# Ordering GpSimd behind VectorE on the shared SBUF port in an attention and MoE kernel

## The chip, the cores and the metric

The kernel runs on one core of a Trainium2 chip. Its time is device time in microseconds (us). Five engines work side by side, each through its own row of instructions: TensorE (PE) for matrix products, VectorE (DVE), ScalarE (ACT), GpSimd (POOL), and SyncE (SP), which here issues DMAs. They wait for each other by semaphores.

## What is computed

Three layers follow each other. The functions of the reference are cut to their cores:

```
# attention with random features, 4 x 8 heads, 576 tokens, 64 wide, 128 features
phi(x) = exp(h - max(h)) / sqrt(m),  h = x @ omega.T - sum(x * x) / 2
kv = phi(k).T @ v;  z = sum(phi(k));  attn = (phi(q) @ kv) / (phi(q) @ z + 1e-6)
# gated layer, 2304 tokens, 512 -> 1536 -> 512
x = (sigmoid(attn @ w_gate) * (attn @ w_val)) @ w_out
# soft mixture: 8 experts with 4 slots each, 512 -> 1024 -> 512
d = softmax(x @ phi, over tokens);  slots = d.T @ x
y = relu(slots[e] @ w1[e]) @ w2[e];  out = softmax(x @ phi, over slots) @ y
```

## The kernel before

The tokens are cut into five blocks of 512 (the last of 256), the gated layer's 1536 columns into twelve chunks. Attention works on 16 units of two heads each (tags `g...`, written to `XT`). For the gated layer each block runs over the chunks: twelve products of 512 columns for the gate (`ga`), twelve for the value (`va`), twelve for the product with w_out (`o`). The mixture's sums are built while later blocks run; its experts come last, from about 635 us.

Products of the gated layer are made of three passes. Each operand is split in a high part (`hi_of`: a copy in a shorter format, on ACT or DVE) and a low part (`lo_of`: a subtraction, mostly on POOL). So before PE can use a weight tile `w`, ACT copies its high part and POOL subtracts the low one. The same is done for `XT`, the attention's output, and for `gt`, the gated values.

During the first 225 us the weights also arrive as 64-bit floats and are converted once (`convert`): two instructions on ACT, then on DVE two TENSOR_SCALAR, one SCALAR_TENSOR_TENSOR (all on `x2T`) and an integer add (`x<-x2T`) that DVE or POOL may make. 36 tiles pass through this, while attention runs too. For the first units POOL also squares the tokens (`g<-g`), which are then summed by DVE.

All of it is recorded first and ordered afterwards. `Plan.schedule` is a planner that runs a list of times: each instruction has a due time, a cost from `Plan.cost`, and the engines on which it may run. `cost` returns a second value, whether the instruction holds the SBUF port that DVE and POOL share: true for every POOL instruction, and for DVE's copies, casts, TENSOR_SCALAR, TENSOR_TENSOR and SCALAR_TENSOR_TENSOR that have no operand in PSUM. While one such instruction is planned to run, `pick` offers the other engine only work that doesn't use the port. `Plan.issue` (line 402) then emits the instructions in the planned order. Each engine keeps that order, but the engines are tied together by data alone: semaphores are set where one reads or overwrites what another wrote. If DVE is behind the plan, POOL goes ahead of it. Nearly all instructions are emitted in line 405, so this line says nothing and the tiles tell the rows apart.

Of the kernel before, what the change touches and what calls it, by code (L numbers as in the profile page):

```python
# [103 lines left out]
class Plan:  # L104
# [294 lines left out]
        assert len(order) == n, (len(order), n)  # L399
        return order  # L400

    def issue(self):
        for _, _, (e, method, a, k) in self.schedule():
            for e, method, a, k in [p[0] for p in k["parts"]] if method == "together" else [(e, method, a, k)]:
                getattr(self.eng[e], method)(*a, **k)  # L405


def body(ctx, tc, nc, qkT, tok, von, omT, wall, phi, w1, w2, ident_d, srep_d, rrep_d, mask_d, out):
    plan = Plan(nc)
    PE, ACT, DVE, POOL, SP = (Eng(plan, e) for e in ("PE", "ACT", "DVE", "POOL", "SP"))  # L410
# [849 lines left out]
    i = 0  # L1260
# [50 lines left out]
        plan.t += 2.0  # L1311
        combine(half, po)
    with tc.manual_schedule():
        plan.issue()


def layout(q, k, v, omega, moe_w_gate, moe_w_val, moe_w_out, moe2_phi, moe2_w1, moe2_w2):
# [42 lines left out]
def build(nc, arrays):  # L1360
    args = [nc.dram_tensor(n, a.shape, mybir.dt.from_np(a.dtype), kind="ExternalInput").ap()
            for n, a in arrays.items()]
    args.append(nc.dram_tensor("out_0", (NTOK, DM), F32, kind="ExternalOutput").ap())
    with tile.TileContext(nc, schedule_with_timeline_sim=True) as tc:
        with ExitStack() as ctx:
            body(ctx, tc, nc, *args)
# [8 lines left out]
```

## Time and profile before

| | us |
|---|---|
| median of 3 runs | 690.68 (690.0 to 691.18) |
| profiled execution, its own time | 688.92 |
| its span in the trace | 687.1 |
| PE busy | 663.6 (97%) |
| DVE busy | 457.7 (67%) |
| ACT busy | 429.0 (62%) |
| POOL busy | 288.7 (42%) |

The span is what the trace covers; the time of the same execution is 1.8 us longer. Busy shares are averages over stages with different limits, and a PE that is busy may still be waiting between two matmuls for less than the trace counts as idle. A row of the timeline has the start in us from the span's start, the duration, the engine, the operation and its tiles (out<-in), shapes and count, and in brackets the idle time of the engine before it and what ended it. Rows of equal instructions that follow each other are put together with one count. [...]

### The profile page before, as it was taken

The page shows a single profiled execution, that of the slowest core. Times are in us where ns is not written, and L with a number is a line of the kernel's source. Part 1 is how long each engine was busy: PE and PEld are TensorE (multiplying, and loading weights), DVE is VectorE, ACT ScalarE, POOL GpSimd, SP SyncE. Part 2 cuts the span into 40 slices and gives each one's busy share as a digit, 9 for nine tenths or more (in the row PEclk, how much of TensorE's full clock was granted, in tenths as well). Part 3 has the DMA queues.
Part 4 walks back from the last instruction along what each step waited for, and adds up shares of the span by engine and source line. Part 5 has one row for each costly group of instructions (what it writes and reads, how often), then busy time and mean ns, then how long its engine had stood idle before and what let it go on. Part 6 is the DMA issues. An engine that isn't in the chain of part 4 may idle for free.

```text
span 687.1 us, 12505 instructions
## 1 busy us (share of the span) xinstructions
PE 663.6 (97%) x4366; PEld 533.8 (78%) x4366; DVE 457.7 (67%) x1299; ACT 429.0 (62%) x962; POOL 288.7 (42%) x245
## 2 busy tenths in 40 slices
PE   7999899999999999999999999999999999999994
PEld 5676577778787888788788888788888789999672
DVE  3899999899997575666666555567444335666413
ACT  5899788888787574766566675554344445675002
POOL 0566445565334343434444543434444444553100
PEclk9999999999999999999999999999999999999997
DMA  8889766777965336443444222589622328666978
GB/s 288 314 271 326 264 208 225 264 251 245 325 239 164 114 125 217 137 133 111 136 155 152 78 62 78 159 299 321 217 93 91 101 71 292 211 203 213 404 287 275
DMA packets 50158, 139.50 MB, mean 203 GB/s; under 512 B 5552, under 2 KB 11184, under 8 KB 50096
## 3 DMA queue, kind: packets, MB, share of 16 engines
q1 hardware_dynamic: 45488, 121.94, 52.2%
q10 hardware_dynamic: 4608, 16.78, 7.2%
q8 instruction: 34, 0.56, 0.3%
q14 instruction: 28, 0.23, 0.1%
HBM read 124.54 MB, written 14.16 MB: 202 GB/s over the span
## 4 chain that ended last, share of the span: by engine, by line
PE 77%; DVE 12%; DMA 4%; ACT 2%; issue 2%; SPq 1%; POOL 0%; DVEq 0%; ACTq 0%
PE o L405 24%; PE ga L405 19%; PE va L405 19%; PE fl L405 15%; DVE x2T L405 4%; DVE g L405 3%; DVE x L405 2%; DMA wscr<-x 1%; DMA g<-in_von 1%; DVE g1b L405 1%; DMA g<-in_tok 1%; ACT ga_a L405 1%; DMA ws<-wscr 1%; DVE ga_a L405 1%; ACT g L405 1%
## 5 line engine op out<-in xcount | busy, mean ns | idle before, releaser
L405 POOL TENSOR_TENSOR w<-ws,w 128x512 fp32r<-128x512 f32 x138 | 181.4, 1315 | 253.2 <-ACT w L405 157.1
L405 PE MATMUL ga<-XT,w 128*128 128x512 f32 (+1 forms) x720 | 168.2, 376 | 1.0 <-DVE ga_a L405 0.9
L405 PE MATMUL va<-XT,w 128*128 128x512 f32 (+1 forms) x720 | 167.3, 375 | 0.4 <-DVE ga_a L405 0.4
L405 PE MATMUL o<-gt,w 128*128 128x512 f32 (+1 forms) x720 | 167.2, 376 | 0.0
L405 PEld LDWEIGHTS va<-XT,w 128*128 128x128 f32 x720 | 123.8, 189 | 26.1 <-issue 3.2
L405 PEld LDWEIGHTS ga<-XT,w 128*128 128x128 f32 x720 | 123.6, 189 | 25.9 <-DVE ga_a L405 1.8
L405 PEld LDWEIGHTS o<-gt,w 128*128 128x128 f32 x720 | 123.5, 189 | 25.3 <-issue 3.9
L405 ACT ACTIVATE w<-ws 128x512 fp32r<-128x512 f32 x107 | 67.2, 628 | 59.4 <-PE o L405 18.9
L405 PE MATMUL fl<-g,g 64*128 64x128 f32 (+4 forms) x686 | 83.8, 313 | 4.9 <-DVE g L405 2.8
L405 ACT ACTIVATE g<-g 128x128 f32<-128x128 f32 (+3 forms) x204 | 73.3, 411 | 14.1 <-DVE g L405 9.1
L405 PEld LDWEIGHTS fl<-g,g 64*128 64x128 f32 (+2 forms) x686 | 60.8, 182 | 26.6 <-DVE g L405 9.1
L405 ACT ACTIVATE ga_a<-ga_a 128x512 f32<-128x512 f32 (+1 forms) x120 | 70.0, 583 | 18.0 <-DVE ga_a L405 17.0
L405 ACT ACTIVATE ga_a<-ga 128x512 f32<-128x512 f32 (+1 forms) x60 | 33.2, 553 | 67.9 <-PE ga L405 67.8
L405 DVE SCALAR_TENSOR_TENSOR ga_a<-ga,ga_a 128x512 f32<-128x512 f32 (+1 forms) x60 | 38.0, 634 | 39.1 <-ACT ga_a L405 39.0
L405 DVE CAST w<-ws 128x512 fp32r<-128x512 f32 x55 | 23.5, 428 | 59.7 <-PE ga L405 41.1
L405 DVE TENSOR_TENSOR ga_a<-va,ga_a 128x512 f32<-128x512 f32 (+1 forms) x60 | 38.1, 634 | 18.7 <-ACT ga_a L405 13.2
L405 ACT ACTIVATE x2T<-g 128x512 f32<-128x512 f32 x72 | 45.5, 665 | 7.8 <-DVE x L405 7.8
L405 ACT ACTIVATE g1b<-g1b,g 128x128 f32<-128x128 f32 x128 | 40.4, 389 | 8.6 <-DVE g L405 8.6
L405 DVE TENSOR_SCALAR x2T<-x2T 128x512 f32<-128x512 f32 (+1 forms) x72 | 44.9, 640 | 0.7 <-ACT x2T L405 0.6
L405 DVE TENSOR_TENSOR gt<-ga_a,gt 128x512 fp32r<-128x512 f32 (+1 forms) x52 | 41.9, 805 | 2.3 <-ACT gt L405 1.3
L405 ACT ACTIVATE ga_a<-ga_a,one_b 128x512 f32<-128x512 f32 (+1 forms) x60 | 40.7, 679 | 2.7 <-issue 1.4
L405 DVE TENSOR_TENSOR g<-fl,g 64x288 f32<-64x288 f32 (+3 forms) x61 | 29.4, 483 | 17.1 <-ACT g L405 16.2
(196 smaller groups left out, 808.0 us busy)
## 6 DMA issues: line engine op xcount, KB each, us to landing
ws<-wscr SPq DMA_DIRECT2D x42, 512.0 KB, 3.6
ws<-wscr SPq DMA_DIRECT2D x78, 256.0 KB, 2.8
g<-in_wall SPq DMA_DIRECT2D x36, 512.0 KB, 4.4
g<-in_von SPq DMA_DIRECT2D x16, 640.0 KB, 6.0
wscr<-x SPq DMA_DIRECT2D x36, 256.0 KB, 3.9
g<-in_qkT SPq DMA_DIRECT2D x15, 576.0 KB, 4.9
g<-in_tok SPq DMA_DIRECT2D x15, 576.0 KB, 4.7
g<-in_w ACTq DMA_DIRECT2D x16, 512.0 KB, 6.0
```

The costliest lines, as they stand in the source:

```text
L405: getattr(self.eng[e], method)(*a, **k)
```

## The change

`issue` now keeps, for each of the two engines, the last emitted instruction that holds the port. When it emits a POOL instruction on the port, and a DVE instruction on the port has been emitted since the last POOL instruction that took one, it adds a dependency: POOL waits for this DVE instruction. Nothing is added in the other direction; DVE never waits for POOL because of the port.

```
--- before.py
+++ after.py
@@ -399,10 +399,18 @@
         assert len(order) == n, (len(order), n)
         return order
 
-    def issue(self):
-        for _, _, (e, method, a, k) in self.schedule():
+    def issue(self, tc):
+
+
+        held = {}
+        sync = mybir.DependencyInfo(mybir.DependencyClass.Sync, mybir.DependencyReason.SCHED_ONLY)
+        for _, i, (e, method, a, k) in self.schedule():
             for e, method, a, k in [p[0] for p in k["parts"]] if method == "together" else [(e, method, a, k)]:
-                getattr(self.eng[e], method)(*a, **k)
+                ins = getattr(self.eng[e], method)(*a, **k)
+            if self.cost(e, method, k, self.ops[i][4], self.ops[i][5])[1]:
+                if e == "POOL" and "DVE" in held:
+                    tc.add_manual_dep(ins.ins, held.pop("DVE").ins.name, sync, reason="port")
+                held[e] = ins
 
 
 def body(ctx, tc, nc, qkT, tok, von, omT, wall, phi, w1, w2, ident_d, srep_d, rrep_d, mask_d, out):
@@ -1311,7 +1319,7 @@
         plan.t += 2.0
         combine(half, po)
     with tc.manual_schedule():
-        plan.issue()
+        plan.issue(tc)
 
 
 def layout(q, k, v, omega, moe_w_gate, moe_w_val, moe_w_out, moe2_phi, moe2_w1, moe2_w2):
```

No engine's row of instructions changes; what changes are the semaphores that stand before POOL's. Here are the rows of POOL at 172 to 216 us, with the semaphores that each waits for, before (`w` is the low part of a weight tile, `ws` its source, `g_78` squares of tokens, `XT` the attention's output; the names in brackets are the engines' semaphores, DMAHW a DMA's):

```order
L405 TENSOR_TENSOR w_269<-ws,w_269 128x512 [waits DMAHW3_49,Activation_49]
L405 TENSOR_TENSOR w_272<-ws,w_272 128x512 [waits DMAHW6_49,PE_49,Activation_49]
L405 TENSOR_TENSOR w_275<-ws,w_275 128x512 [waits Activation_49]
L405 TENSOR_TENSOR w_277<-ws,w_277 128x512 [waits DMAHW1_49,Activation_49]
L405 TENSOR_TENSOR w_282<-ws,w_282 128x512 [waits DMAHW4_49,PE_49,Activation_49]
L405 TENSOR_TENSOR w_285<-ws,w_285 128x512 [waits Activation_49]
L405 TENSOR_TENSOR w_287<-ws,w_287 128x512 [waits DMAHW7_49,Activation_49]
L405 TENSOR_TENSOR w_295<-ws,w_295 128x512 [waits DMAHW3_49,Activation_49]
L405 TENSOR_TENSOR g_78<-g_78 128x512 [waits DVE_49]
L405 TENSOR_TENSOR w_297<-ws,w_297 128x512 [waits DMAHW6_49,Activation_49]
L405 TENSOR_TENSOR w_303<-ws,w_303 128x512 [waits DMAHW3_49,PE_49,Activation_49]
L405 TENSOR_TENSOR XT<-g_80,XT 128x288 [waits Activation_49]
```

and the same rows of POOL after the change:

```order
L409 TENSOR_TENSOR w_269<-ws,w_269 128x512 [waits DMAHW3_49,DVE_49,Activation_49]
L409 TENSOR_TENSOR w_272<-ws,w_272 128x512 [waits DVE_49,DMAHW6_49,PE_49,Activation_49]
L409 TENSOR_TENSOR w_275<-ws,w_275 128x512 [waits DVE_49,Activation_49]
L409 TENSOR_TENSOR w_277<-ws,w_277 128x512 [waits DMAHW1_49,DVE_49,Activation_49]
L409 TENSOR_TENSOR w_282<-ws,w_282 128x512 [waits DVE_49,DMAHW4_49,PE_49,Activation_49]
L409 TENSOR_TENSOR w_285<-ws,w_285 128x512 [waits DVE_49,Activation_49]
L409 TENSOR_TENSOR w_287<-ws,w_287 128x512 [waits DMAHW7_49,DVE_49,Activation_49]
L409 TENSOR_TENSOR w_295<-ws,w_295 128x512 [waits DMAHW3_49,DVE_49,Activation_49]
L409 TENSOR_TENSOR g_78<-g_78 128x512 [waits DVE_49]
L409 TENSOR_TENSOR w_297<-ws,w_297 128x512 [waits DMAHW6_49,DVE_49,Activation_49]
L409 TENSOR_TENSOR w_303<-ws,w_303 128x512 [waits DVE_49,DMAHW3_49,PE_49,Activation_49]
L409 TENSOR_TENSOR XT<-g_80,XT 128x288 [waits DVE_49,Activation_49]
```

The order is the same, and eleven of the twelve now wait for DVE as well.

## Rows read from the trace of the kernel before

**Rows 1.** The page's first part: busy us (share of span) and instructions.
```profile
PE 663.6 (97%) x4366; PEld 533.8 (78%) x4366; DVE 457.7 (67%) x1299; ACT 429.0 (62%) x962; POOL 288.7 (42%) x245
```

**Rows 2.** Stretches of 25 us: their length, busy us (instructions) by engine, PEclk, DMA.
```profile
175.00:200.00 25.00, 23.83 (x125) 19.18 (x124) 24.93 (x51) 19.95 (x41) 8.67 (x7) 1.00 0.80 281
...
475.00:500.00 25.00, 25.00 (x140) 20.38 (x139) 13.12 (x27) 11.43 (x20) 11.61 (x9) 1.00 0.67 238
```

**Rows 3.** PE's waits, 25 to 225 us: total us, times, longest.
```profile
PE fl L405 <- DVE g L405: 5.7, 7, 1.7
PE ga L405 <- DVE ga_a L405: 0.7, 1, 0.7
PE o L405 <- DVE g L405: 0.5, 1, 0.5
```

**Rows 4.** PE's timeline at six of these waits.
```profile
79.98 0.37 PE L405 MATMUL fl<-g,g 64*128 64x128 f32 x1 [0.24 <-DVE g L405]
...
85.02 0.38 PE L405 MATMUL fl<-g,g1b 128*128 128x128 f32 x1 [1.70 <-DVE g L405]
...
104.44 0.38 PE L405 MATMUL fl<-g,g 128*128 128x128 f32 x1 [0.32 <-DVE g L405]
...
185.41 0.33 PE L405 MATMUL fl<-ident,g 128*128 128x128 f32 x1 [0.53 <-DVE g L405]
...
189.25 0.33 PE L405 MATMUL fl<-ident,g 128*128 128x128 f32 x1 [0.64 <-DVE g L405]
...
209.44 0.51 PE L405 MATMUL fl<-g,g 128*128 128x288 f32 x1 [1.65 <-DVE g L405]
```

**Rows 5.** DVE's groups by shape, 50 to 225 us: count, busy us, mean ns, idle before.
```profile
L405 DVE CUSTOM_DVE_ANT_0 x<-x2T 128x1024 uint16<-128x1024 uint16 x24 | 23.4, 975 | 0.1
L405 DVE TENSOR_SCALAR x2T<-x2T 128x512 f32<-128x512 f32 x32 | 20.8, 661 | 0.0
...
L405 DVE CUSTOM_DVE_ANT_0 g1b<-fl,g 128x128 f32<-128x128 f32 x48 | 10.6, 281 | 0.5 <-PE fl L405 0.5
```

**Rows 6.** DVE's and POOL's timeline, 174 to 189 us.
```profile
174.01 0.68 DVE L405 CUSTOM_DVE_ANT_0 x<-x2T 128x1024 uint16<-128x1024 uint16 x1
...
182.40 1.78 DVE L405 CUSTOM_DVE_ANT_0 x<-x2T 128x1024 uint16<-128x1024 uint16 x1
184.10 0.41 DVE L405 TENSOR_SCALAR x2T<-x2T 128x512 int32<-128x512 int32 x1
184.44 0.28 DVE L405 CUSTOM_DVE_ANT_0 g1b<-fl,g 128x128 f32<-128x128 f32 x1
...
186.85 1.79 DVE L405 CUSTOM_DVE_ANT_0 x<-x2T 128x1024 uint16<-128x1024 uint16 x1
...
182.07 1.55 POOL L405 TENSOR_TENSOR w<-ws,w 128x512 fp32r<-128x512 f32 x1 [2.94 <-ACT w L405]
186.80 1.30 POOL L405 TENSOR_TENSOR w<-ws,w 128x512 fp32r<-128x512 f32 x1 [3.18 <-ACT w L405]
```

**Rows 7.** DVE's timeline before the two longest waits.
```profile
80.94 3.19 DVE L405 TENSOR_SCALAR x2T<-x2T 128x512 f32<-128x512 f32 x3
...
206.64 1.78 DVE L405 CUSTOM_DVE_ANT_0 x<-x2T 128x1024 uint16<-128x1024 uint16 x1
```

**Rows 8.** POOL, DVE and PE around 164 us.
```profile
164.22 1.74 POOL L405 TENSOR_TENSOR w<-ws,w 128x512 fp32r<-128x512 f32 x1
...
167.03 1.52 DVE L405 TENSOR_SCALAR x2T<-x2T 128x512 f32<-128x512 f32 x1
...
168.22 2.88 PE L405 MATMUL o<-gt,w 128*128 128x512 f32 x12
```

**Rows 9.** POOL, DVE and PE around 58 us.
```profile
57.78 1.07 POOL L405 TENSOR_TENSOR XT<-g,XT 128x224 fp32r<-128x224 f32 x1
...
59.09 0.81 DVE L405 CUSTOM_DVE_ANT_0 x<-x2T 128x1024 uint16<-128x1024 uint16 x1
...
60.01 0.63 PE L405 MATMUL ga<-XT,w 128*128 128x512 f32 x2
```

## The prediction

> **What bounds the kernel now.** I read four views in this order: the page's busy times, the stretches of 25 us, the waits of TensorE, and the rows of VectorE and GpSimd around the places where TensorE stands still. TensorE (PE) is busy 97% of the span [rows 1], so only what it loses can be won. The stretches show where it loses. From 475 to 500 us, as in nearly every stretch from 225 to 575, PE is busy 25.00 of 25.00 us and VectorE (DVE) only 13.12: there PE sets the pace, and a later GpSimd (POOL) instruction costs nothing as long as PE's next input is ready. From 50 to 225 us it is the other way round: in the stretch from 175 DVE is busy 24.93 us and PE 23.83 [rows 2]. This is where weights are converted and two things share VectorE: conversion and attention.
>
> The waits say the same. Between 25 and 225 us PE waits 5.7 + 0.7 + 0.5 = 6.9 us for DVE, in nine places [rows 3]; six of them, from 80 to 210 us, sum to 0.24 + 1.70 + 0.32 + 0.53 + 0.64 + 1.65 = 5.08 us [rows 4]. So the question is why DVE is late in these six places.
>
> It is late because some of its instructions take over a microsecond longer than they need. The correction step (x<-x2T, the custom add) takes 0.68 us where nothing else touches the port [rows 6], but 975 ns on average over its 24 instances between 50 and 225 us; TENSOR_SCALAR on x2T, 0.41 us alone [rows 6], takes 661 [rows 5]. The long instances are all of one kind: POOL has begun a TENSOR_TENSOR a moment before. POOL starts at 186.80 and takes 1.30 us; DVE's add starts at 186.85 and takes 1.79 instead of 0.68, that is, it ends 0.54 us after POOL does [rows 6]. So DVE stands for the whole of POOL's instruction. If DVE is first, POOL pays, and far less: POOL's instruction that began at 182.07, during a DVE instruction, took 1.55 us against 1.30 [rows 6].
>
> **What the change does, and its price.** No instruction is added, removed or moved to another place in its engine's row; POOL gets waits. Of its 245 instructions 97 wait for DVE before and 183 after. The wait is for the DVE instruction on the port that stands just ahead in the plan. I set beside each POOL start in the trace the end of the DVE instruction it will wait for, plus 0.08 us, which is what passes in this trace between the end of a DVE instruction and the start of a POOL instruction that waited for it: 68 POOL instructions would start at least 0.1 us later, 38 of them between 50 and 225 us, by up to 6.3 us. The other new waits are over when POOL comes to them and cost nothing.
>
> *Gain on DVE.* Take the two collisions shown. POOL's instruction of 182.07 (its next DVE instruction, 182.40, took 1.78 us) and that of 186.80 will wait for the DVE instruction behind the blocked one. So both adds take 0.68 us, and DVE is 2 x 1.10 = 2.20 us ahead. Then POOL runs. Whether DVE now stands for it, one instruction later, depends on what DVE has next. At 184.44 come seven custom instructions of 0.28 us that read PSUM (g1b<-fl) [rows 6]; instructions that read PSUM are not lengthened in this trace (the average of the 48 such instances between 50 and 225 us is 281 ns [rows 5]). They cover POOL's 1.3 us. At 80.94 it is the same, and larger: three TENSOR_SCALARs take 3.19 us instead of 3 x 0.41 while POOL runs four instructions [rows 7]; POOL's first will come after all three, under eight custom instructions. At 206.64 the add takes 1.78 us behind POOL [rows 7]; that POOL instruction will wait for a later add, at 209.91. Each of the six waits of PE has 1.0 us or more of such loss in the ten or so DVE instructions before it, the longest (1.70 us) has the 3.19 us of these rows. I count 71 DVE instructions that lose over 0.2 us at the port, 50 us together; 25 of them, 22 us, are blocked by a POOL instruction that will now wait for them or for a later one. That is four times PE's six waits.
>
> *Gain on PE.* I take the six waits as gone: 5.08 us. Each costs a little more than its idle time: 12 matmuls of 512 columns in a row take 2.88 us and a single one 0.38, so they start (2.88 - 0.38) / 11 = 0.23 us apart [rows 8], and 0.15 us of overlap is lost at each stop. Six times 0.15 is 0.90, together 5.98 us. The three waits before 80 us (1.8 us in all) I leave out: the blocked instructions ahead of them are short or are not behind a new wait.
>
> *Cost.* Behind each waiting POOL instruction stand its other ones: the low parts of the weights (w), which PE needs, the squares and XT. The tightest place is at 164.22 [rows 8]. That instruction makes the low part of the third weight tile; it will wait for the TENSOR_SCALAR that ends at 167.03 + 1.52 = 168.55, and so start 4.4 us later. PE reads its result at the third matmul of the row that begins at 168.22, at 168.68; POOL ended at 165.96, so the slack is 2.7 us and PE would stop for 1.7. But 1.1 us of that TENSOR_SCALAR's 1.52 is itself time blocked by the next POOL instruction, which now cannot begin before it. That leaves 0.6. Elsewhere between 164 and 207 us the slack is 3 to 7 us and about as large as the delay or larger. At 57.78 an XT part will wait for the add that ends at 59.09 + 0.81 = 59.90, and start 2.2 us later; it ended at 58.85 and PE reads it at 60.01 [rows 9], so the loss is up to 1.0. I take 0.6 us of cost in all; its bounds are 0, if DVE's gain pulls every wait forward, and 1.7 + 1.0 = 2.7 us if it gains nothing. The wait itself costs at most its 0.08 us on an engine that is busy 42% [rows 1].
>
> Net: 5.98 - 0.6 = 5.4 us. The profiled execution took 688.92 us (span 687.1, the rest around it), below the three timed runs; against it the sum is 683.5, against their median of 690.68 it is 685.3.
>
> **A rule that speaks against it.** Rows 6 show that one instruction stands until the other is done, and that the first one wins. [...] By that rule a wait only changes who is first, and the port's own queueing is replaced by a semaphore's. If the two orders cost the same, nothing is won. The trace disagrees on the last step: DVE loses 1.10 us when it is second, POOL 0.25 when it is second.
>
> **The rivals.**
>
> *The block moves on.* POOL starts 0.08 us after its partner, and DVE's next instruction, if it uses the port, meets it there. Where the conversion's four to six instructions stand in an unbroken row (DVE from 165 to 182 us has few that read PSUM), the loss of 1.1 us comes back one or two instructions later. This speaks for it: 46 of the 71 blocked instructions are blocked by a POOL instruction that no new wait holds back behind them. Then PE's six waits stay: 690.7 us, or 688.8 if one of the two long ones (1.65 or 1.70, and 0.15) goes after all.
>
> *POOL becomes the late one: slower.* If DVE gains nothing, its queue reaches the partners no earlier than in this trace, and POOL's delays stand at full size. PE then waits for the w of 164.22 and the XT of 57.78: 2.7 us, 693.4. It decides when a delay passes the slack of PE's next read (2.7 us at 164.22). Against it: the long delays are made of the blocked time that the waits remove.
>
> *Nothing happens,* because the waits are already satisfied: 690.7 us. The 68 late starts speak against it.
>
> **How the numbers follow.** About 0.2%, 1.4 us, is what a measurement can tell from no change. The forecast, 685.3, has 0.74; its own range goes from 683.0 (the three early waits gone too, no cost: 5.98 + 1.8 = 7.7) to 687.4 (gain 6.0, cost 2.7). The moved block has 0.14, half of it at 688.8 and so over 0.2% faster; POOL late 0.08; nothing 0.04. Faster: 0.74 + 0.07 = 0.81. Same: 0.07 + 0.04 = 0.11. Slower: 0.08. The range from 683.0 to 690.0 leaves out the slower case, the upper part of the same ones and little below.
>
> **What would show it.** If it is right, the custom adds and TENSOR_SCALARs between 50 and 225 us average nearer to 0.75 and 0.50 us; PE's waits for DVE from 80 to 210 us are gone; POOL waits for DVE far more; and from 225 us on the program runs as before, 5 to 6 us earlier. If instead DVE's averages stay, the block has moved on. If PE waits for POOL's w between 150 and 215 us, the second rival holds. The prediction is wrong if the chip does not hand POOL the port between two DVE instructions that follow each other closely, since POOL will now always arrive in such a place.

## The result and the profile after

The changed kernel takes 683.63 us (median of four runs, 682.83 to 683.66) against 690.45 for the kernel before in the same comparison (690.0 to 691.18): a ratio of 0.9898 with a 95% interval of 0.9881 to 0.9914, so 6.8 us less. The forecast was 5.4 us less, 685.3. The profiled execution of the changed kernel took 683.61 us with a span of 681.4; the profiled one of before took 688.92, which is under all of its timed runs, and so the two traces differ by 5.3 us in their times.

The page's first part, to be read beside rows 1, gives busy us, share of the span and instructions:

```profile
PE 661.9 (97%) x4366; PEld 533.8 (78%) x4366; DVE 439.6 (65%) x1299; ACT 428.5 (63%) x962; POOL 283.4 (42%) x245
```

DVE does the same 1299 instructions in 18.1 us less (457.7 before). POOL does its 245 in 5.3 us less: its XT parts of 128x224 average 699 ns instead of 796, its squares of 128x640 1262 instead of 1347.

The stretches of 25 us, with the columns of rows 2:

```profile
175.00:200.00 25.00, 25.00 (x126) 20.29 (x125) 24.90 (x60) 20.13 (x42) 9.84 (x8) 1.00 0.90 306
200.00:225.00 25.00, 25.00 (x145) 20.62 (x144) 17.41 (x54) 19.00 (x44) 12.44 (x11) 1.00 0.53 164
```

PE is now busy 25.00 us in the stretch from 175, where it had 23.83. DVE is still full there (24.90 us), but gets 60 instructions done in it instead of 51. In the stretch from 200 it has time to spare. PE's granted clock is 1.00 in both, as it was in before.

PE's timeline from 20 to 226 us of the changed kernel, those rows that begin after an idle time (in brackets, with what ended it); it answers rows 3 and 4:

```profile
28.38 0.49 PE L409 MATMUL ga<-XT,w 128*128 128x512 f32 x1 [0.30 <-POOL w L409]
...
33.20 0.71 PE L409 MATMUL o<-g,g 128*64 128x288 f32 x4 [0.36 <-DVE g L409]
...
34.73 1.97 PE L409 MATMUL fl<-g,g 128*128 128x256 f32 x8 [0.83 <-DVE g L409]
...
44.30 1.74 PE L409 MATMUL o<-g,g 128*128 128x256 f32 x8 [0.25 <-DVE g L409]
...
64.49 2.11 PE L409 MATMUL ga<-XT,w 128*128 128x512 f32 x8 [1.01 <-DVE ga_a L409]
```

After 64.49 us there is none. All six stops of rows 4 are gone. Ahead of 80 us five stops stand where there were three, and they come to 0.30 + 0.36 + 0.83 + 0.25 + 1.01 = 2.75 us, where they were 1.8. The one at 28.38, for POOL's `w`, is new.

DVE's groups by shape from 50 to 225 us answer rows 5; first two groups of the kernel before that are not among them, then the changed kernel:

```profile
L405 DVE SCALAR_TENSOR_TENSOR x2T<-g,x2T 128x512 int32<-128x512 int32 x32 | 27.7, 864 | 0.1
...
L405 DVE TENSOR_SCALAR x2T<-x2T 128x512 int32<-128x512 int32 x32 | 20.3, 638 | 0.1
```

```profile
L409 DVE SCALAR_TENSOR_TENSOR x2T<-g,x2T 128x512 int32<-128x512 int32 x32 | 27.2, 850 | 0.1
L409 DVE CUSTOM_DVE_ANT_0 x<-x2T 128x1024 uint16<-128x1024 uint16 x24 | 19.8, 824 | 0.1
L409 DVE TENSOR_SCALAR x2T<-x2T 128x512 f32<-128x512 f32 x32 | 17.4, 553 | 2.1 <-ACT x2T L409 2.1
L409 DVE TENSOR_SCALAR x2T<-x2T 128x512 int32<-128x512 int32 x32 | 16.1, 506 | 0.1
...
L409 DVE CUSTOM_DVE_ANT_0 g1b<-fl,g 128x128 f32<-128x128 f32 x48 | 10.6, 282 | 0.2 <-PE fl L409 0.2
```

The add went from 975 to 824 ns, the two TENSOR_SCALARs from 661 to 553 and from 638 to 506. The SCALAR_TENSOR_TENSOR stayed (864 and 850). Undisturbed, the add and the SCALAR_TENSOR_TENSOR take 0.68 us and a TENSOR_SCALAR 0.41 ([rows 6] for two of them; all four are seen undisturbed in e6 below, at 688 and 422 ns). What lies above that, times the count, is what DVE lost at the port in these groups: before 32 x 0.184 + 24 x 0.295 + 32 x 0.251 + 32 x 0.228 = 28.3 us, after 16.5. This sum serves as the measure in the experiments. It covers these four groups alone, not all of DVE's instructions.

How it looks in one place: the three TENSOR_SCALARs of rows 7 and what follows, on DVE, POOL and PE of the changed kernel. It is the place of the stop of 1.70 us.

```profile
79.60 1.09 DVE L409 TENSOR_SCALAR x2T<-x2T 128x512 f32<-128x512 f32 x3
80.62 0.29 DVE L409 CUSTOM_DVE_ANT_0 g1b<-fl,g 128x128 f32<-128x128 f32 x1
...
80.83 1.30 POOL L409 TENSOR_TENSOR w<-x,w 128x512 fp32r<-128x512 f32 x1 [1.16 <-DVE x2T L409]
82.09 1.42 POOL L409 TENSOR_TENSOR XT<-g,XT 128x288 fp32r<-128x288 f32 x2
...
80.53 1.88 PE L409 MATMUL ga<-XT,w 128*128 128x512 f32 x7
82.25 0.94 PE L409 MATMUL fl<-g,g1b 128*128 128x128 f32 x7
```

The three take 1.09 us instead of 3.19. POOL, released by DVE's x2T, runs beside the custom instructions that read PSUM and lengthens none of them (0.29 and, on average, 0.282 us). PE reaches its product with g1b at 82.25 without a stop; it was at 85.02 [rows 4].

The start of the same matmul in both traces shows where the gain comes in:

| place, us in before | start after | earlier by | gained since the row above |
|---|---|---|---|
| 70.09 | 70.03 | 0.06 | 0.06 |
| 80.34, behind the stop at 79.98 | 79.65 | 0.70 | 0.64 |
| 85.02 | 82.25 | 2.78 | 2.08 |
| 104.76, behind the stop at 104.44 | 101.30 | 3.46 | 0.68 |
| 168.22 | 164.51 | 3.71 | 0.25 |
| 185.41 | 181.04 | 4.37 | 0.66 |
| 189.25 | 184.03 | 5.22 | 0.85 |
| 209.44 | 202.37 | 7.07 | 1.85 |
| 571.44 | 564.07 | 7.37 | 0.30 |
| 677.75, the last matmul | 672.03 | 5.72 | -1.65 |

The gain is made between 80 and 210 us, kept to 571, and 1.65 us of it is lost in the gated layer's last block, from 575 to 630 us. PE's rows of that loss, first of before, then of the changed kernel:

```profile
587.95 1.69 PE L405 MATMUL ga<-XT,w 128*128 128x256 f32 x12 [0.25 <-DVE ga_a L405]
589.92 0.33 PE L405 MATMUL fl<-ident,x2T 128*128 128x128 f32 x1 [0.28 <-ACT x L405]
```

```profile
580.95 1.69 PE L409 MATMUL ga<-XT,w 128*128 128x256 f32 x12 [0.61 <-DVE ga_a L409]
583.42 0.33 PE L409 MATMUL fl<-ident,x2T 128*128 128x128 f32 x1 [0.78 <-ACT x L409]
...
623.33 1.08 PE L409 MATMUL fl<-dt,acc 128*128 128x32 f32 x8 [0.58 <-DVE mx L409]
```

The third of these stops isn't there in before.

### The profile page after: what moved, and what is told of

It is laid out like the page before. It is cut to its first block, busy times and chain, and to the rows that moved or that the text cites. A ratio compares the mean times of both kernels' runs of the same rounds, so it can differ in the third digit from the quotient of the medians.

```text
span 681.4 us, 12554 instructions
## 1 busy us (share of the span) xinstructions
PE 661.9 (97%) x4366; PEld 533.8 (78%) x4366; DVE 439.6 (65%) x1299; ACT 428.5 (63%) x962; POOL 283.4 (42%) x245
## 4 chain that ended last, share of the span: by engine, by line
PE 84%; DMA 6%; DVE 3%; ACT 2%; POOL 1%; issue 1%; SPq 1%; DVEq 0%; ACTq 0%; POOLq 0%
PE o L409 25%; PE ga L409 22%; PE va L409 21%; PE fl L409 17%; DMA ws<-wscr 3%; DMA g<-in_tok 1%; DVE g L409 1%; DMA g<-in_von 1%; ACT g L409 1%; ACT ga_a L409 1%; SPq L409 1%; DMA wscr<-x 1%; POOL w L409 1%; POOL g L409 1%; DVE w L409 0%
## 5 line engine op out<-in xcount | busy, mean ns | idle before, releaser
L409 ACT ACTIVATE w<-ws 128x512 fp32r<-128x512 f32 x107 | 67.3, 629 | 62.0 <-PE o L409 19.1
L409 DVE TENSOR_SCALAR x2T<-x2T 128x512 f32<-128x512 f32 (+1 forms) x72 | 37.5, 533 | 2.8 <-ACT x2T L409 2.7
L409 POOL TENSOR_TENSOR XT<-g,XT 128x64 fp32r<-128x64 f32 (+2 forms) x43 | 28.6, 681 | 24.0 <-ACT ga_a L409 6.3
```

Source lines behind the costliest of these rows:

```text
L409: ins = getattr(self.eng[e], method)(*a, **k)
```

## The experiments

The theory: from 75 to 225 us DVE sets the pace, and what pays is that DVE no longer stands for a whole POOL instruction while POOL, which has slack, waits in its place. The rivals: the gain comes from the later waits as well, or is lost through them; a fixed order on the port would do, whoever waits; the less the two meet, the better, at whatever price in waiting. Every diff is against the changed kernel. The measure "DVE lost" is the sum worked out above; times of before are those measured beside each run.

| run | us (runs) | before beside it | ratio (95%) | DVE lost at the port, us | DVE idle for POOL in the same four groups, us |
|---|---|---|---|---|---|
| before | | | | 28.3 | 0 |
| after | 683.63 (4) | 690.45 | 0.9898 (0.9881 to 0.9914) | 16.5 | 0 |
| e1_early | 684.08 (6) | 689.99 | 0.9914 (0.9896 to 0.9933) | 18.4 | 0 |
| e2_late | 689.36 (12) | 689.99 | 0.9992 (0.9981 to 1.0002) | 28.4 | 0 |
| e3_one | 687.41 (8) | 689.99 | 0.9960 (0.9946 to 0.9974) | 26.6 | 0 |
| e4_any | 690.62 (12) | 689.99 | 1.0007 (0.9994 to 1.0020) | 20.4 | 0 |
| e5_reverse | 694.12 (12) | 690.6 | 1.0048 (1.0028 to 1.0068) | 19.1 | 9.0 |
| e6_both | 690.75 (12) | 690.6 | 1.0007 (0.9989 to 1.0024) | 1.2 | 28.5 |
| e7_prev | 681.82 (6) | 690.6 | 0.9877 (0.9848 to 0.9906) | 16.0 | 0 |

### One place alone

The waits are left to five POOL instructions only, those from 76.63 to 83.81 us, ahead of the stop of 1.70 us. In the trace POOL waits for DVE 99 times, against 97 in before: two of the five get a wait that they didn't have.

```
+        n = 0
-                if e == "POOL" and "DVE" in held:
+                n += e == "POOL"
+                if e == "POOL" and "DVE" in held and 32 < n <= 37:
```

> New waits for five GpSimd instructions only, those at 76.63 to 83.81 us in the trace of before. Theory (a wait of TensorE goes when the blocked VectorE instructions just ahead of it go): the two waits of 0.24 and 1.70 us that end at 79.98 and 85.02 disappear, with 0.15 us each, and nothing else: 690.5 - 2.2 = 688.3 us. Rival (the block moves on to a later VectorE instruction before TensorE's next wait): TensorE loses at 104 or 185 us what it won at 85, and the time is 690.5 us.

Measured: 687.41 us against 689.99, 2.6 us less. In its trace PE is 0.52 us earlier than in before at 70.09, 3.05 earlier at 85.02, and 3.18 at 573: the 2.5 us come in at this place and stay. DVE's and PE's rows there:

```profile
79.32 1.09 DVE L410 TENSOR_SCALAR x2T<-x2T 128x512 f32<-128x512 f32 x3
...
81.97 1.05 PE L410 MATMUL fl<-g,g1b 128*128 128x128 f32 x8
...
182.24 0.66 PE L410 MATMUL fl<-ident,g 128*128 128x128 f32 x4 [0.55 <-DVE g L410]
186.09 0.66 PE L410 MATMUL fl<-ident,g 128*128 128x128 f32 x4 [0.66 <-DVE g L410]
206.25 1.31 PE L410 MATMUL fl<-g,g 128*128 128x288 f32 x4 [1.64 <-DVE g L410]
```

The stops with waits are gone, the others stand with their old size (0.53, 0.64 and 1.65 in rows 4). So these two stops go where POOL's waits are, and the gain of this place isn't taken back at the next.

### The conversion stage or the rest

e1 keeps the waits up to about 230 us, the first 95 POOL instructions on the port; e2 keeps only those behind. The diffs are as above with `n <= 95` and `n > 95`.

> The new waits are kept for the first 95 GpSimd instructions on the port, those up to about 230 us, and left out for all later ones. Theory: the gain is made in the conversion stage alone (TensorE is 7.1 us ahead at 226 us in the changed kernel), and the waits of the last block cost 1.6 us (TensorE is 7.4 us ahead at 575 us and 5.7 at 630), because a later GpSimd instruction frees a weight buffer later and the next load comes later. So this kernel keeps the one and drops the other: 682.0 us, 8.4 below before. Rival: the 1.6 us lost late is not the waits' doing, but follows from the earlier finish of the conversion meeting other transfers: then 683.6 us, as the changed kernel.

> The other half alone: new waits only for the GpSimd instructions after the 95th, from about 230 us on. Theory: nothing is gained, and the last block loses the same 1.6 us: 692.0 us against 690.5 before. Rival (the late loss comes from being early, not from the waits): 690.5 us, within 0.2% of before. Rival (the gain is made all over the program): below 690 us.

Measured: 684.08 and 689.36 us, both against 689.99. The late waits alone give nothing that can be told from zero. PE's waits from 25 to 225 us in e2, with the columns of rows 3, are those of before:

```profile
PE fl L410 <- DVE g L410: 5.7, 7, 1.7
PE ga L410 <- DVE ga_a L410: 0.7, 1, 0.7
PE o L410 <- DVE g L410: 0.5, 1, 0.5
```

In e1's trace PE gains 7.12 us between 70 and 226 us, in the changed kernel's 7.09, and from there to 571 us e1 gains nothing and the changed kernel 0.2. So the gain is made in the stage where DVE was the bound. Leaving the late waits out was to give 1.6 us back, since the changed kernel's trace loses 1.65 in the last block; it gave none, and e1's own trace loses 0.65 us there without a single wait in that block. A second comparison of e1 came to the same:

> The waits of the changed kernel for the first 95 GpSimd instructions alone, once more, beside the two others on the same chip. Theory: the waits of the last block cost 0.9 us (its length in the four profiles of programs without waits of this kind there is about 0.9 below that in the three with them), so 0.9 us below the changed kernel, 682.9 us. Rival (the last block's length varies by itself with the landing of its weight loads): 683.7 us, as the changed kernel.

Measured: 684.21 us (six runs, 681.86 to 686.12). This is 1.3 us above what was expected if the late waits cost time: the times show no cost of them.

### DVE waits instead of POOL

The mirror image: a DVE instruction on the port waits for the POOL instruction that the plan has ahead of it, and POOL gets no new wait.

```
-                if e == "POOL" and "DVE" in held:
-                    tc.add_manual_dep(ins.ins, held.pop("DVE").ins.name, sync, reason="port")
+                if e == "DVE" and "POOL" in held:
+                    tc.add_manual_dep(ins.ins, held.pop("POOL").ins.name, sync, reason="port")
```

> The mirror image: VectorE waits for the GpSimd instruction on the port that stands ahead of it in the plan, and GpSimd gets no new wait. Theory (VectorE sets the pace up to 225 us; VectorE must not stand for GpSimd, and when it does the price is the whole 1.1 us): VectorE now stands for GpSimd even where GpSimd is late, the six waits of TensorE grow: 692 to 696 us. Rival (what pays is that the two engines follow the planned order, whichever waits): faster than before by 2 us or more.

Measured: 694.12 us, 3.5 us more than before (690.6). DVE's groups from 50 to 225 us, the last column being idle time ahead of the instructions and what ended it, and PE's waits from 25 to 225:

```profile
L409 DVE SCALAR_TENSOR_TENSOR x2T<-g,x2T 128x512 int32<-128x512 int32 x32 | 25.9, 808 | 1.8 <-POOL w L409 1.3 <-POOL x L409 0.3
...
L409 DVE TENSOR_SCALAR x2T<-x2T 128x512 int32<-128x512 int32 x32 | 18.2, 571 | 4.9 <-POOL w L409 3.6 <-POOL x L409 1.2
...
PE fl L409 <- DVE g L409: 5.8, 9, 1.7
PE ga L409 <- DVE ga_a L409: 2.3, 2, 1.7
```

In these four groups DVE loses 9.2 us less at the port and stands 9.0 us for POOL instead: 28.1 us in all, as before. Over all of DVE's instructions from 50 to 225 us the waits for POOL come to 12.0 us, so DVE is worse off on the whole, and PE's stops from 25 to 225 us come to 9.2 us against 6.9 in before. A fixed order alone is worth nothing here; it matters who waits.

### Both wait

Both of these conditions stand in the loop, so that the two never meet on the port.

```
+                if e == "DVE" and "POOL" in held:
+                    tc.add_manual_dep(ins.ins, held.pop("POOL").ins.name, sync, reason="port")
```

> Each of the two engines waits for the other's instruction on the port that stands ahead of it in the plan, so the port is used in the planned order throughout. Theory: the gain of the changed kernel (6 to 7 us) less what VectorE loses by standing for a late GpSimd, 3 to 4 us: about 687.5 us. Rival (the planned order itself is what pays): 683.5 us or below.

Measured: 690.75 us against 690.6: no gain, and 3 us more than was expected. DVE's groups from 50 to 225 us:

```profile
L409 DVE SCALAR_TENSOR_TENSOR x2T<-g,x2T 128x512 int32<-128x512 int32 x32 | 22.0, 688 | 9.5 <-POOL w L409 7.0 <-POOL g L409 1.3 <-POOL XT L409 0.8
L409 DVE CUSTOM_DVE_ANT_0 x<-x2T 128x1024 uint16<-128x1024 uint16 x25 | 17.2, 688 | 7.0 <-POOL w L409 5.1 <-POOL g L409 1.1 <-POOL XT L409 0.8
L409 DVE TENSOR_SCALAR x2T<-x2T 128x512 int32<-128x512 int32 x32 | 13.4, 422 | 7.4 <-POOL w L409 5.9 <-POOL x L409 1.2 <-POOL XT L409 0.4
L409 DVE TENSOR_SCALAR x2T<-x2T 128x512 f32<-128x512 f32 x32 | 13.1, 421 | 4.6 <-POOL w L409 1.7 <-POOL gt L409 1.4 <-POOL g L409 1.4
```

All four groups run at their undisturbed length: nothing is blocked any more. And DVE is idle for 28.5 us ahead of them, where it had lost 28.3 to blocking. One place, DVE and POOL:

```profile
171.88 0.42 DVE L409 TENSOR_SCALAR x2T<-x2T 128x512 int32<-128x512 int32 x1
172.21 0.69 DVE L409 TENSOR_TENSOR ga_a<-va,ga_a 128x512 f32<-128x512 f32 x1
173.78 0.69 DVE L409 SCALAR_TENSOR_TENSOR x2T<-g,x2T 128x512 int32<-128x512 int32 x1 [0.88 <-POOL w L409]
...
172.44 1.30 POOL L409 TENSOR_TENSOR w<-ws,w 128x512 fp32r<-128x512 f32 x1 [1.21 <-DVE x2T L409]
```

POOL starts behind its partner, DVE has one instruction that reads PSUM to put beside it, and then stands 0.88 us until POOL is done at 173.74. For this sum it makes no difference whether DVE stands in its instruction or ahead of it. From [rows 6] the prediction worked out, as what speaks against the change, that a semaphore would only take the place of the port's own queue. For waits in both directions the traces agree with that, 28.3 us lost in before against 28.5 of idle time here. With waits on POOL alone it doesn't come out so, 16.5.

That the time is that of before is a sum of several things. Against before, PE gains 1.9 us between 70 and 226 us in this trace, where it gains 7.1 in the changed kernel, and it loses 1.75 between 26 and 70 us and 2.7 from 571 us to the end.

### Which instruction POOL waits for

e4 lets POOL wait for the last DVE instruction of any kind, also those that read PSUM, which `cost` doesn't count as users of the port (of these, the ones that write g1b take 281 ns on average in before [rows 5] and 282 in the changed kernel). e7 lets it wait for the DVE instruction on the port one earlier than the change does.

```
-            if self.cost(e, method, k, self.ops[i][4], self.ops[i][5])[1]:
+            if e == "DVE" or self.cost(e, method, k, self.ops[i][4], self.ops[i][5])[1]:
```

```
-                    tc.add_manual_dep(ins.ins, held.pop("DVE").ins.name, sync, reason="port")
+                    held.pop("DVE")
+                    if held.get("OLD"):
+                        tc.add_manual_dep(ins.ins, held.pop("OLD").ins.name, sync, reason="port")
+                if e == "DVE":
+                    held["OLD"] = last
+                    last = ins
```

> GpSimd waits for the last VectorE instruction of any kind that stands before it in the plan, and not for the last one on the port; more waits, and later ones. Theory (what pays is that GpSimd runs beside VectorE instructions that read PSUM, and these stand right behind the port instruction it waits for): those instructions now come first, GpSimd meets the next port instruction, and its results come later than TensorE's slack allows: the gain is gone, 689 to 693 us. Rival (what pays is that VectorE goes first, wherever): the gain stays, 683 to 685 us.

> GpSimd waits for one instruction earlier: not for the last VectorE instruction on the port ahead of it in the plan, but for the one on the port before that. Theory: GpSimd then arrives 0.08 us after that one ended, when VectorE has already begun the last one; GpSimd stands at the port for its 0.4 to 0.7 us and runs right after it, beside the same instructions that read PSUM. So the gain is the same to within 0.5 us, 683 to 684.5 us, and GpSimd's instructions get longer by 0.2 to 0.5 us each where VectorE is behind the plan. Rival (the exact partner matters, since GpSimd now gets the port before the last one does): half the gain or more goes, 687 us or above.

e4 measured 690.62 us against 689.99: the whole gain is gone. These are the rows of PE, from 20 to 226 us, that come behind an idle time that POOL ended:

```profile
29.19 0.50 PE L409 MATMUL ga<-XT,w 128*128 128x512 f32 x1 [1.08 <-POOL w L409]
...
62.42 0.73 PE L409 MATMUL ga<-XT,w 128*128 128x512 f32 x2 [0.77 <-POOL XT L409]
...
172.07 2.57 PE L409 MATMUL ga<-XT,w 128*128 128x512 f32 x10 [0.22 <-POOL w L409]
```

DVE still loses 7.9 us less at the port than before (20.4), but POOL's waits are now so late that PE stops for POOL's own results, w and XT: 0.30 us of that in the changed kernel, 1.08 + 0.77 + 0.22 = 2.07 here. At 62.42 it is the XT of rows 9: against before, PE is 1.32 us late at 57.12 and 2.40 late here, where the changed kernel is 0.04 late. The f32 TENSOR_SCALARs even average 734 ns, above the 661 of before; that POOL, released behind an instruction that reads PSUM, then runs beside what follows it, would explain that, but is only argued. Between 70 and 226 us PE still gains 2.8 us against before; between 26 and 70 it loses 2.2. This is the second rival of the prediction, made true by a stronger wait.

e7 measured 681.82 us against 690.6, better than the 683 to 684.5 that were expected. Its trace has only the three early stops of before left, at 30.14, 34.95 and 64.03 us (0.51, 0.62 and 0.75 us), and its f32 TENSOR_SCALARs average 471 ns.

Whether the earlier partner is truly better was asked with three more runs: the changed kernel again beside e7 (e8), e7's waits up to 230 us alone (e9), and e7 again (e11), these two beside e10.

> The changed kernel once more, beside the others on the same chip, so that differences of under 1 us can be read: 683.6 us by its first four runs. The first 30 us of these programs start between 0.7 us earlier and 1.0 later from run to run, with the arrival of the first inputs; a result between 682.8 and 684.5 us would be in keeping with that.

> The waits for one instruction earlier (as in the run of that kind), but only for the first 95 GpSimd instructions on the port, up to about 230 us. Theory: the gain of the conversion stage stays and the last block, from 575 us, loses nothing to waits: within 0.5 us of the kernel with such waits throughout, since there the last block lost next to nothing either. Rival (the late waits for one instruction earlier are what made that kernel 2 us faster than the changed one): 2 us slower than that kernel.

> The kernel with waits for one instruction earlier, once more. It took 681.8 us, 2.0 below the changed kernel beside it, where less than 0.5 was expected. If that difference is the kernel's, 681.3 to 682.5 us again, and 2 us below the early waits of the other kind; if it came from the run, 683 to 684.

Measured: 683.86 us for the changed kernel (six runs; ratio 0.9901, 0.9874 to 0.9928), 683.28 for the early half of e7 (six; 0.9902, 0.9879 to 0.9926), 682.91 for e7 (five; 0.9895, 0.9878 to 0.9912). e7 was 2.0 us below the changed kernel beside it; e11 was 1.3 below e10, and e9 0.9. The intervals overlap in every comparison, so the times leave open how much better e7 is.

The traces say more. Between 70 and 226 us PE gains 7.1 us (7.06 to 7.16) against before in all seven traces with waits of either kind up to 226 us (the changed kernel twice, e1, e10, e7, e9, e11). There it doesn't matter which of the two partners POOL waits for. Between 26 and 70 us the three with the earlier partner gain 0.46 to 0.48 us, the four with the later one between -0.21 and 0.15. So e7 is better by 0.3 to 0.7 us in that early stretch; the rest of its advantage comes from the first 26 us and from the last block, which vary from one execution to the next. An instruction on the port earlier is as good or a little better; a later one, e4, takes the gain away.

## Why the prediction was right

**What bounds the kernel.** Right, and now shown: e2 leaves the stage before 230 us as it was and gains nothing that can be told from zero, e1 changes only that stage and gains 5.9 us.

**The gain on DVE.** The count was 25 instructions with 22 us, and about 21 us of that lie between 25 and 225 us. DVE's busy time fell by 18.1 us in the whole program, but for the instructions of this stretch only by 11.8. So about half of the time counted was won there. The averages of the add and of TENSOR_SCALAR were to be nearer to 0.75 and 0.50 us: 0.824 and 0.553, from 0.975 and 0.661. That DVE would not stand for POOL elsewhere, because POOL would run beside instructions that read PSUM, holds at 80.83 us (0.28 us each beside it, as without it). It doesn't hold everywhere: of 28.3 us lost 16.5 remain. Of the instructions between 25 and 225 us that take over 0.2 us longer than undisturbed, 46 in before, 29 lose less than that now; but 14 others that ran freely before are blocked now, for 9.8 us together. In the unbroken rows of conversion between 165 and 180 us, the place that the first rival named, the block did move on:

```profile
168.28 1.30 POOL L409 TENSOR_TENSOR w<-ws,w 128x512 fp32r<-128x512 f32 x1 [1.03 <-ACT w L409]
...
168.65 1.48 DVE L409 SCALAR_TENSOR_TENSOR x2T<-g,x2T 128x512 int32<-128x512 int32 x1
```

POOL's wait for DVE was over here when its last operand came from ACT. The rival's mechanism is there then, with its price (1.48 us instead of 0.68), and the prediction left it out of its sum. There is enough time won on DVE around it that PE doesn't stop.

**The gain on PE.** The six stops were all taken as gone, with 0.15 us of overlap each, 5.98 us. They are gone, and the steps of the table at these places are 0.64, 2.08, 0.68, 0.66, 0.85 and 1.85 us, 6.76 together. With what is gained between them and behind 210 us (0.06 + 0.25 + 0.30) it is 7.37 to 571 us. This term was 1.4 us too small. About half of that is the overlap: a stop cost some 0.27 us beyond its idle time, not 0.15 (at 85.02 the gain at the stop of 1.70 is 1.87 us, and 0.11 more comes with the next matmuls). The rest is places with no idle time in the rows, 0.18 us each at 70.7 and 144.6 us and 0.2 at 290. Leaving out the three stops ahead of 80 us was right: idle time there even grew.

**The cost.** Taken at 0.6 with bounds of 0 and 2.7. At rows 8 it is 0. POOL's instruction starts at 163.33 instead of 164.22, since DVE is itself ahead, and the wait that ends last is the one for ACT. But it is close:

```profile
163.33 1.48 POOL L409 TENSOR_TENSOR w<-ws,w 128x512 fp32r<-128x512 f32 x1 [2.68 <-ACT w L409]
...
164.51 2.91 PE L409 MATMUL o<-gt,w 128*128 128x512 f32 x12
```

POOL ends at 164.81. PE's third matmul of the row reads the result two steps of 0.23 us in, at 164.97; the slack of 2.7 us has shrunk to 0.16. At rows 9 PE comes out 0.04 us late instead of 0.12 early, so 0.16 us went there. Over the whole stretch from 26 to 70 us, the new stop for POOL's `w` included, PE loses 0.2 us against before; in the other three traces with these waits it is between 0.1 lost and 0.15 gained.

**From 225 us on.** "The program runs as before, 5 to 6 us earlier": this step failed in this pair of traces. It runs 7.4 us earlier to 571 us, and 1.65 us goes in the last block. From the product at 571 us to the end the trace of before is the shortest of those looked at; in the four traces without new late waits between 0.5 and 1.6 us go too (e3 0.5, e1 0.65, e10 1.15, e9 1.6), in those with late waits on POOL between 0.7 and 2.7. So a part of the 1.65 may be the luck of before's profiled execution, which was 1.8 us under the median of its runs. Whether the late waits cost the rest was asked with e1 and e10 against the changed kernel, and the times (684.08 and 684.21 against 683.63 and 683.86) say no. What exactly makes the last block longer in one execution than in another stays open.

So the net sum of 5.4 us was 2.0 short of the 7.4 that PE is ahead at 571 us: 1.4 in the gain and the 0.6 taken off as cost, of which 0.16 is seen at one place. Against the profiled execution that is hidden by the 1.65 us of the last block: 5.3 us between the two profiled executions, 5.4 forecast. The mechanism was right, but this closeness is luck. The medians are 6.8 apart, 1.4 more than forecast.

## What to carry to other kernels

When two engines share a port and the trace shows that the second one stands for the whole of the first one's instruction, let the engine with slack wait for the one that sets the pace, in this direction only, and choose the wait such that it then runs beside work that doesn't use the port. Here waits in both directions turned blocked time into idle time one to one (28.3 us into 28.5), and waits on the busy engine did no better (19.1 us blocked and 9.0 idle); so before adding such a wait, add up what the busy engine loses at the port and check that the waiting one's readers have slack. A gain in such a stage is to be read at the stops of the engine that bounds the whole, since of 11.8 us won at the port 7.1 reached PE by the end of the stage.

## What the hardware showed that was not expected

With waits on both sides the collisions went to nothing (688 and 422 ns, the undisturbed lengths) and the time didn't move by a measurable amount (ratio 1.0007): what DVE had lost in its instructions, 28.3 us, it now stood ahead of them, 28.5.

At one place of the changed kernel POOL gets the port between two DVE instructions that follow each other closely, and pays 0.44 us for it (1.74 instead of 1.30). It is the second of two POOL instructions in a row, the first of which comes 0.10 us behind the start of a DVE instruction at 172.04, the second 0.20 behind that of 173.63:

```profile
172.04 0.69 DVE L409 SCALAR_TENSOR_TENSOR x2T<-g,x2T 128x512 int32<-128x512 int32 x1
...
173.63 0.79 DVE L409 CUSTOM_DVE_ANT_0 x<-x2T 128x1024 uint16<-128x1024 uint16 x1
174.34 1.52 DVE L409 TENSOR_SCALAR x2T<-x2T 128x512 f32<-128x512 f32 x1
...
172.14 3.44 POOL L409 TENSOR_TENSOR w<-ws,w 128x512 fp32r<-128x512 f32 x2 [2.56 <-ACT ga_a L409]
```

The two take 3.44 us, against 2 x 1.30 undisturbed: 0.84 us for both, where a DVE instruction that comes second loses 1.1 alone. The second runs from 173.83 to 175.58 and gets the port ahead of the TENSOR_SCALAR of 174.34, which starts as the add of 173.63 ends (174.42) and takes 1.52 us instead of 0.41. So POOL isn't kept out here, and the price, 1.11 us, falls on the next DVE instruction on the port.
